# Last pair's g in six buffers, other places for the passes' first loads, and one rounding moved in the first paired step

## The chip, the cores and the metric

The kernel runs on one core of one Trainium2 chip. The time is device microseconds of one execution. Three runs of the kernel before took 910.87, 908.1 and 909.05 us, so the median is 909.05 us.

## The reference

Windowed attention (4 heads with a plain window of 32 keys, 4 with a dilated one), then a dense layer pair without any gating by experts:

```python
def _moe_ref(x, w_in, w_out):
    h = x @ w_in                                              # 4608 x 512 by 512 x 2048
    sp = np.maximum(h, 0.0) + np.log1p(np.exp(-np.abs(h)))    # softplus
    g = h * erf(sp)
    return (g @ w_out).astype(np.float32)                     # by 2048 x 512

def reference(**kwargs):
    attn_out = _attn_ref(q, k, v)          # B, H, S, D = 8, 8, 576, 64
    x = attn_out.transpose(0, 2, 1, 3).reshape(B * S, H * D)
    return _moe_ref(x, w_in, w_out)
```

Inputs and output are float32.

## The kernel before

Matrix products in float32 are made of three products of rounded parts: a value is split into `hi` (rounded) and `lo` (the residue), and hi·hi + hi·lo + lo·hi is summed in PSUM. A cast makes `hi` (mostly on ACT), a subtraction on DVE makes `lo`.

The 4608 tokens are nine chunks of 512. Attention runs in the first part, between the dense work of chunks 0 to 2, and its rest beside the first pair. Chunks 3 to 8 are taken in three pairs, A and B. A pair's first product x·w_in is done by seven block products in place of eight (sums and differences of blocks on both sides), in eight *steps* d of 256 features; seven products a step of six matmuls each. `mm1_big` issues product k, and `take_big` adds its result from PSUM into the step's four half tiles: A's and B's g buffers, of two halves of 512 columns each. Product 0 is copied by ACT into A's second half (L806); products 1 to 6 are added on DVE (L804 and, for both halves of B at once, L816). Then ACT makes softplus (L829) and erf (L1182), and DVE multiplies (L833): the buffer then holds g.

For the first two pairs the steps run in `period`, interleaved with the second product g·w_out of older items (24 matmuls in four quarters, L642), with what is left of attention and with the preparation of x's block sums; `third` issues a group of products. `split_item` rounds an item's g into `ghi` and `glo`. The first paired step is period 0.

The last pair's eight steps (d = 16 to 23, called steps 0 to 7 here) run in `final`, with nothing interleaved on PE. Their g goes to DRAM: A's to a tensor `ga`, B's to one of the tensors `g`, one step later (`store_g`, issued from ACT's queue). The product's operands on the left are loaded two steps ahead by `load_left` (win<-ws, in two parts). Small jobs for later stand in two tables: `LATE` (at a step's end) and `HALFWAY` (after its fifth product).

`rest_steps` then does the second product of the last two items of the pair before ("rest items": 48 matmuls), and `store` writes that chunk from the four PSUM banks `acc`. The last pair's own second product is done by `sums_step`, sixteen *passes* s, again with seven block products (42 matmuls of 256 columns a pass). Each pass needs a half tile of g from two steps: `load_e` fetches it back, `row_sums` makes the block sums on DVE, `operands` rounds them (L1112 on ACT, L968 on DVE). Operands of pass s + 2 are made during pass s, and the load for pass s + 4 is issued at its end. The right-hand block sums of w_out (tensors `wd`) are loaded by `load_sums(p)`, p = 0 to 6; pass s uses p = 2(s mod 4) and the one after it.

Everything runs in the order in which the code issues it (`manual_schedule`): each engine and each DMA queue works its list from the front, and an instruction that waits holds all behind it. SP's queue carries all loads and the output; ACT's queue carries the stores of the last pair's g. Pools hand out buffers in turn: a new tile of a name waits until the tile that had its buffer `bufs` allocations ago is no longer used, also by a store that still reads it. Names that matter: `hc` (two buffers of 1024 columns), `slab(0)` and `slab(1)` (the tiles dbl0 and dbl1 as such buffers), `ghi` and `glo` (two of 512 each), `w` (four of 512).

Before, `pair_of` gives the last pair's even steps the two slabs and its odd ones the two `hc`, so a buffer comes again after two steps. Pass 0 is loaded into two `w` at the end of step 2, pass 1 into slab(1) at the end of step 7, and pass 2 into an `hc` after all matmuls of the rest items.

## Time and profile before

| | |
|---|---|
| median of three runs | 909.05 us |
| the profiled execution, own time | 912.83 us |
| its span, first to last instruction | 911.0 us |
| mean granted clock of PE | 0.985 |
| PE busy | 873.6 us |
| DVE busy | 696.4 us |
| ACT busy | 609.3 us |
| DMA | 193.02 MB, mean 212 GB/s |

A row of the timeline has the start, the duration, the engine, the source line, the operation, out<-in by the program's names and the count of merged instructions; in brackets stand the idle time of the engine ahead of it and what ended that. Matmuls are pipelined, so the start-to-start distance is what a matmul costs. Rows of the chain of work that ended last have a start, a duration and who held it: an engine with its line, a DMA, or "issue". Rows of the table by windows have the window, its length, the busy time of PE, the weight loads, DVE, ACT and POOL with counts, then PE's granted clock (1.00 is full speed), the busy share of the sixteen DMA engines and GB/s. The span by stage: first paired step at 355 us, last pair's steps from 713 us, rest items from 804 us, passes from 815 us.

### The profile page before, as it was taken

How to read it: one execution, taken by the hardware profiler on the slowest of the kernel's cores; microseconds unless marked ns; L12 is line 12 of the kernel's file. 1: busy time of each engine (PE TensorE's matmuls, PEld its weight loads, DVE VectorE, ACT ScalarE, POOL GpSimd, SP SyncE). 2: the span in 40 equal slices, each digit the busy share in tenths (PEclk: the TensorE clock that was granted, in tenths of full speed). 3: DMA queues.
4: the chain of work that ended last, by engine and by line, in shares of the span. 5: the costliest groups of instructions: out<-in, count | busy, mean ns of one | idle time of the engine just before them, and what ended most of it. 6: DMA issues, size and time to landing. Idle time of an engine off the chain costs nothing.

```text
span 911.0 us, 21918 instructions
## 1 busy us (share of the span) xinstructions
PE 873.6 (96%) x8410; PEld 715.4 (79%) x8422; DVE 696.4 (76%) x1748; ACT 609.3 (67%) x1356; POOL 78.6 (9%) x97
## 2 busy tenths in 40 slices
PE   7789999999999999999999999999999988896998
PEld 3467888888888888788888888888888866686998
DVE  5788988887788788686677765868887667675885
ACT  6889989887887887466758525664665456663442
POOL 2212101111111110000110000000000000000000
PEclk9899999999999999999999999999999999997999
DMA  7874436562858887466666825566686388858331
GB/s 277 283 252 147 146 124 209 182 201 89 273 184 304 299 301 241 164 226 219 223 208 229 306 82 188 206 207 196 214 287 250 100 291 271 292 199 301 117 122 64
DMA packets 82568, 193.02 MB, mean 212 GB/s; under 512 B 8992, under 2 KB 25632, under 8 KB 79392
## 3 DMA queue, kind: packets, MB, share of 16 engines
q1 hardware_dynamic: 80160, 183.24, 59.7%
q10 hardware_dynamic: 2304, 8.39, 2.3%
q8 instruction: 66, 1.08, 0.5%
q14 instruction: 38, 0.31, 0.1%
HBM read 133.92 MB, written 57.67 MB: 210 GB/s over the span
## 4 chain that ended last, share of the span: by engine, by line
PE 81%; DMA 9%; DVE 4%; ACT 4%; issue 2%; SPq 1%; POOL 0%; DVEq 0%; ACTq 0%; POOLq 0%
PE acc L642 31%; PE h L796 8%; PE tx L796 8%; PE h L527 7%; PE tx L527 7%; PE acc L1135 4%; PE sp L796 3%; PE sp L281 3%; PE sp L223 2%; PE sp L1135 2%; DMA g<-hc 2%; DMA g<-dbl 2%; DMA ga<-hc 2%; DMA v<-in_v_dram 1%; PE sp L262 1%
## 5 line engine op out<-in xcount | busy, mean ns | idle before, releaser
L642 PE MATMUL acc<-wout_hi,ghi 128*128 128x512 f32 x448 | 177.6, 396 | 0.0
L642 PE MATMUL acc<-wout_lo,ghi 128*128 128x512 f32 x448 | 175.0, 391 | 0.0
L642 PE MATMUL acc<-wout_hi,glo 128*128 128x512 f32 x448 | 124.6, 392 | 0.0
L257 POOL TENSOR_TENSOR prob<-prob,rinv 128x256 f32<-128x256 f32 x72 | 72.0, 1006 | 476.5 <-DVE ssum L255 240.5
L244 ACT ACTIVATE prob<-prob,nmax 128x64 f32<-128x64 f32 x288 | 96.4, 338 | 10.9 <-DVE nmax L234 10.6
L642 PEld LDWEIGHTS acc<-wout_hi,glo 128*128 128x128 f32 x448 | 84.7, 189 | 18.1
L642 PEld LDWEIGHTS acc<-wout_hi,ghi 128*128 128x128 f32 x448 | 84.3, 188 | 17.0 <-DVE ghi L617 0.4
L642 PEld LDWEIGHTS acc<-wout_lo,ghi 128*128 128x128 f32 x448 | 84.4, 188 | 16.8
L234 DVE CUSTOM_DVE_ANT_0 prob<-sp,cst 128x64 f32<-128x64 f32 x288 | 45.2, 220 | 42.5 <-ACT rows L323 29.1
L829 ACT ACT_TABLE_LOAD x26 | 33.4, 1283 | 54.9 <-DVE dbl L804 28.8
L796 PE MATMUL tx<-win 128*128 128x512 f32 x216 | 55.8, 394 | 0.4 <-DVE dbl L816 0.4
L796 PE MATMUL h<-win 128*128 128x512 f32 x216 | 55.7, 393 | 0.0
L244 ACT ACTIVATION_READ_ACCUMULATOR prob<-prob,nmax 128x1 f32 x288 | 54.7, 190 | 0.0
L527 PE MATMUL h<-x,win 128*128 128x512 f32 x192 | 48.7, 396 | 0.0
L527 PE MATMUL tx<-x,win 128*128 128x512 f32 x192 | 48.0, 392 | 0.0
L796 PEld LDWEIGHTS tx<-win 128*128 128x128 f32 x216 | 39.9, 188 | 9.6 <-DVE dbl L816 0.8
L323 ACT COPY rows<-sp 128x128 f32<-128x128 f32 (+7 forms) x167 | 27.6, 309 | 29.7 <-PE sp L223 29.3
L796 PEld LDWEIGHTS h<-win 128*128 128x128 f32 x216 | 39.9, 188 | 9.2 <-DVE dbl L806 0.7
L829 ACT ACTIVATE s<-dbl 128x1024 f32<-128x1024 f32 x24 | 25.4, 1060 | 27.9 <-DVE dbl L804 27.8
L527 PEld LDWEIGHTS h<-x,win 128*128 128x128 f32 x192 | 35.4, 188 | 8.0
L527 PEld LDWEIGHTS tx<-x,win 128*128 128x128 f32 x192 | 35.7, 188 | 7.5
L281 PEld LDWEIGHTS sp<-pT,v 64*64 64x64 f32 x1824 | 29.4, 134 | 11.1 <-DVE s L611 4.6
(311 smaller groups left out, 1948.9 us busy)
## 6 DMA issues: line engine op xcount, KB each, us to landing
win<-ws SPq DMA_DIRECT2D x24, 1024.0 KB, 5.5
v<-in_v_dram SPq DMA_DIRECT2D x72, 256.0 KB, 5.3
win<-ws SPq DMA_DIRECT2D x24, 768.0 KB, 5.8
qk<-in_qk_dram SPq DMA_DIRECT2D x48, 272.0 KB, 5.0
dbl<-in_w_in_dram SPq DMA_DIRECT2D x16, 512.0 KB, 4.0
dbl<-in_w_out_dram SPq DMA_DIRECT2D x16, 512.0 KB, 4.0
ws<-x SPq DMA_DIRECT2D x32, 256.0 KB, 4.9
win<-wd SPq DMA_DIRECT2D x14, 512.0 KB, 7.9
```

The costliest lines, as they stand in the source:

```text
L223: nc.tensor.matmul(sps[h][r * STRIP:(r + 1) * STRIP, i, p, :], qkz[i][hs, s * STRIP:(s + 1) * STRIP], qkz[i][hs, at:at + KEYS], start=True ...
L234: nc.vector.tensor_tensor_reduce(out=pr[:, g, :], in0=sps[h][:, u % 2, p, :], in1=mask[QUADS.index(kinds(u, p))], scale=-SCALE, scalar=HUG ...
L244: nc.scalar.activation(out=probs[u][:, j, :], in_=probs[u][:, j, :], func=AF.Exp, scale=-1.0, bias=nmax[:, j:j + 1], accum_out=sums[u][:, ...
L257: nc.gpsimd.tensor_tensor(probs[u], probs[u], rinv.broadcast_to([P, 2 * PARTS, KEYS]), op=ALU.mult)
L262: nc.tensor.transpose(out=turn_place(u)[:, h * P:(h + 1) * P], in_=pr[:, PARTS * h:PARTS * (h + 1), :].rearrange("p a k -> p (a k)"), iden ...
L281: nc.tensor.matmul(xp[h * D:(h + 1) * D, qs], vt[ks, s, h, :], pt[ks, h * P + s * STRIP:h * P + (s + 1) * STRIP], start=True, stop=True, t ...
L323: nc.scalar.copy(out=to, in_=src)
L527: nc.tensor.matmul((h, bank)[j], win_at[:, ftp, j, cc // 2, w, cc % 2, :], x[cc], start=(k == 0 and i == 0), stop=(k == CC - 1 and i == 2))
L642: nc.tensor.matmul(args["out"], args["lhsT"], args["rhs"], start=args["start"], stop=args["stop"])
L796: nc.tensor.matmul(bank_, w[:, wi, c, :], x[c][:, xi, :], start=(c == 0 and n == 0), stop=(c == 1 and n == 2))
L829: nc.scalar.activation(out=ls[kind_, d], in_=hs[kind_, d], func=AF.Softplus)
L1135: nc.tensor.matmul(y, x[:, at_], w, start=(q == 0 and j == 0 and n == 0), stop=(q == QUART - 1 and j == 1 and n == 2))
```

## The change

Three things change.

1. **Six buffers.** `pair_of` gives the last pair's steps in turn the slabs, the `hc` pair, and four separate tiles of 512 columns, `ghi` twice for A and `glo` twice for B (steps 2 and 5). For these, softplus, multiply and store are issued in halves, and product 5 is added in two instructions.
2. **The passes' first loads.** Pass 0's load, sums and operands come a step later, its operands partly halfway in a step, and the load of the rest items stands halfway in step 6. Pass 1 is loaded into two `w` halfway in step 7. Pass 2 is loaded into slab(1) while the rest items are multiplied. The chunk that the rest items end is written from two `w`, `o` and a `glo`. Later passes go round slab(1), slab(0) and the two `hc` in another order.
3. **First paired step.** The residue of B22 (`LO["B22"]`, two subtractions) is issued ahead of products 4 and 5; the multiply of item NT - 1 and the rounding of its first half come behind them.

```diff
-    def store(c):
+    def store(c, outs=None):
...
-            if c == 0:
+            if outs:
+                o = outs[tt]
+                copy_for(tt)(out=o, in_=acc[tt])
+            elif c == 0:
...
+    def seg(e, j):
+        return e[j] if isinstance(e, list) else e[:, j]
+    def spans(e, *others):
+        if isinstance(e, list):
+            return [(e[j], *(o[:, j] for o in others)) for j in range(PAIR)]
+        return [(e, *others)]
...
+        elif k == 5 and isinstance(hs["B", d], list):
+            add(b0, b0)
+            add(b1, b1)
...
     def pair_of(d):
-        if d % 2:
+        if d >= FIN * SPC and (d - FIN * SPC) % 3 == 2:
+            return [[work.tile([P, TOK], F32, name=n) for _ in range(PAIR)] for n in ("ghi", "glo")]
+        if (d - FIN * SPC) % 3 if d >= FIN * SPC else d % 2:
             return [work.tile([P, PAIR, TOK], F32, name="hc") for _ in range(2)][::-1]
         return [slab(i) for i in range(2)]
...
-            nc.scalar.activation(out=ls[kind_, d], in_=hs[kind_, d], func=AF.Softplus)
+            for e, l in spans(hs[kind_, d], ls[kind_, d]):
+                nc.scalar.activation(out=l, in_=e, func=AF.Softplus)
...
     def store_g(kind_, d, queue):
-        queue.dma_start(out=kept_g[kind_, d // SPC][d % SPC], in_=hs[kind_, d])
+        for e, g in spans(hs[kind_, d], kept_g[kind_, d // SPC][d % SPC]):
+            queue.dma_start(out=g, in_=e)
...
-        if i == 0:
-            multiply(NT - 1)
-        elif behind_ is not None and not ended:
+        if behind_ is not None and not ended:
             multiply_big("A", behind_)
...
-        if ahead is not None:
+        if ahead is not None and i:
             split_item(ahead, 0)
+        if i == 0:
+            jobs(AFT.get((i, 2), ()))
...
         third(2)
-        jobs(AFT.get((i, 2), ()))
+        if i == 0:
+            multiply(NT - 1)
+            split_item(ahead, 0)
+        else:
+            jobs(AFT.get((i, 2), ()))
...
     def room_e(s):
-        return work.tile([P, PAIR, TOK], F32, name="hc") if s % 2 else slab(1 - s // 2 % 2)
+        return slab(s % 2) if s % 4 in (1, 2) else work.tile([P, PAIR, TOK], F32, name="hc")
...
-    LATE = {0: [(sub_split, 6), (sub_store, 6)], 1: [(sub_whole, 7)], 2: [(sub_sums, 7), (load_e, 0, room_halves)],
-            3: [(row_sums, 0, room_w)], 4: [(operands, 0, 0), (operands, 0, 1)],
-            5: [(operands, 0, 2), (operands, 0, 3), (load_rest,)], 6: [(load_sums, 0), (load_sums, 1)],
-            7: [(load_e, 1, lambda: slab(1)), (load_sums, 2), (load_sums, 3)]}
-    HALFWAY = {7: [(split_rest, 0, 0), (split_rest, 0, 1)]}
+    LATE = {0: [(sub_split, 6), (sub_store, 6)], 1: [(sub_whole, 7)], 2: [(sub_sums, 7)],
+            3: [(load_e, 0, room_halves)], 4: [(row_sums, 0, room_w)], 5: [(operands, 0, 1)],
+            6: [(load_sums, 0), (load_sums, 1)], 7: [(load_sums, 2), (load_sums, 3)]}
+    HALFWAY = {5: [(operands, 0, 0)], 6: [(operands, 0, 2), (operands, 0, 3), (load_rest,)],
+               7: [(split_rest, 0, 0), (split_rest, 0, 1), (load_e, 1, room_halves)]}
...
                 load_sums(4)
+                load_e(2, lambda: slab(1))
...
-        load_e(2, lambda: work.tile([P, PAIR, TOK], F32, name="hc"))
-        store(done(REST[-1]))
+        store(done(REST[-1]), [io.tile([P, TOK], F32, name="w", bufs=4) for _ in range(2)] +
+              [small.tile([P, DM], F32, name="o", bufs=1), work.tile([P, TOK], F32, name="glo")])
         load_sums(5)
         load_sums(6)
```

What this does to the order is seen at three places. A row has the source line, the operation, out<-in and what it waits for: DMAHW is a transfer, the others are engines. Line numbers of the change are those of its own file.

ACT around the start of step 2, before (L806 is the copy of a step's first product, L1182 erf, L829 softplus; dbl_8669 is slab(0), dbl_8670 slab(1)):

```order
L806 COPY dbl_8669<-sp_90 128x512 [waits DMAHW5_49,PE_49]
L1182 ACT_TABLE_LOAD
L1182 ACTIVATE s<-s 128x1024 [waits Activation_49] x2
L839 DMA ga<-hc 128x1024 [waits DMAHW1_49,DVE_49]
L829 ACT_TABLE_LOAD [waits DVE_49]
L829 ACTIVATE s<-dbl_8669 128x1024 [waits Activation_49]
L839 DMA g_114<-hc 128x1024 [waits DMAHW4_49,DVE_49]
L829 ACTIVATE s<-dbl_8670 128x1024 [waits DVE_49,Activation_49]
L806 COPY hc<-tx 128x512 [waits DMAHW1_49,PE_49]
```

And now:

```order
L818 COPY ghi<-sp_90 128x512 [waits PE_49]
L1206 ACT_TABLE_LOAD
L1206 ACTIVATE s<-s 128x1024 [waits Activation_49] x2
L859 DMA ga<-hc 128x1024 [waits DMAHW1_49,DVE_49]
L848 ACT_TABLE_LOAD
L848 ACTIVATE s<-ghi 128x512 [waits Activation_49]
L848 ACTIVATE s<-ghi 128x512 [waits DVE_49]
L859 DMA g_114<-hc 128x1024 [waits DMAHW3_49,DVE_49]
L848 ACTIVATE s<-glo 128x512 [waits DVE_49,Activation_49]
L848 ACTIVATE s<-glo 128x512
L818 COPY dbl_8741<-tx 128x512 [waits DMAHW5_49,PE_49]
```

Step 2's copy goes to a `ghi` and waits for PE alone; step 3's copy goes to slab(0) and waits for step 0's store (DMAHW5), no longer for step 1's; softplus comes in halves.

SP's queue from the last load of sums that stands ahead of the output (win<-wd), before (L1051 is a load for a pass, L680 the output):

```order
L1031 DMA win<-wd 128x1024 [waits DMAHW7_49,PE_49]
L1051 DMA hc<-ga 128x2x256 [waits DMAHW4_49,DMAHW0_49,DVE_49]
L1051 DMA hc<-ga 128x2x256 [waits DMAHW1_49]
L680 DMA out_dram<-o 128x512 [waits DMAHW2_49,DVE_49]
L680 DMA out_dram<-w 128x512 [waits DMAHW3_49,Activation_49]
L680 DMA out_dram<-w 128x512 [waits DVE_49]
L680 DMA out_dram<-w 128x512 [waits DMAHW5_49,Activation_49]
L1031 DMA win<-wd 128x1024 [waits DMAHW6_49,PE_49]
```

And now (dbl_9160 is slab(1)):

```order
L1055 DMA win<-wd 128x1024 [waits DMAHW1_49,PE_49]
L1075 DMA dbl_9160<-ga 128x2x256 [waits DMAHW5_49,DMAHW3_49,DVE_49]
L1075 DMA dbl_9160<-ga 128x2x256
L683 DMA out_dram<-w 128x512 [waits DMAHW6_49,DVE_49]
L683 DMA out_dram<-w 128x512 [waits DMAHW7_49,Activation_49]
L683 DMA out_dram<-o 128x512 [waits DMAHW0_49,DVE_49]
L683 DMA out_dram<-glo 128x512 [waits DMAHW1_49,Activation_49]
L1055 DMA win<-wd 128x1024 [waits DMAHW2_49,PE_49]
```

The place in the queue is the same; the buffer that pass 2's load waits for is another one, left by step 6 and not by step 7.

DVE in the first paired step, before (L804 and L816 take products 4 and 5, L740 makes the residue of B22, L266 copies the turned probabilities that the values on PE need):

```order
L611 TENSOR_TENSOR hc<-hc,s 128x1024 [waits Activation_49]
L617 CAST ghi<-hc 128x512 [waits DVE_49,PE_49]
L618 TENSOR_TENSOR glo<-hc,ghi 128x512 [waits DVE_49,PE_49]
L804 TENSOR_TENSOR dbl_5089<-h,dbl_5090 128x512 [waits PE_49]
L816 TENSOR_TENSOR dbl_5090<-tx,dbl_5090 128x1024 [waits DVE_49,PE_49]
L740 TENSOR_TENSOR dbl_5067<-dbl_5067 128x512 [waits DMAHW3_49,DMAHW1_49,Activation_49]
L740 TENSOR_TENSOR plain<-plain 128x512 [waits DMAHW4_49,DMAHW2_49,Activation_49]
L266 COPY pT_87<-sp_90 128x256 [waits PE_49]
```

And now:

```order
L743 TENSOR_TENSOR dbl_5067<-dbl_5067 128x512 [waits DMAHW3_49,DMAHW1_49,Activation_49]
L743 TENSOR_TENSOR plain<-plain 128x512 [waits DMAHW4_49,DMAHW2_49,Activation_49]
L816 TENSOR_TENSOR dbl_5089<-h,dbl_5090 128x512 [waits DVE_49,PE_49]
L832 TENSOR_TENSOR dbl_5090<-tx,dbl_5090 128x1024 [waits DVE_49,PE_49]
L611 TENSOR_TENSOR hc<-hc,s 128x1024
L617 CAST ghi<-hc 128x512 [waits DVE_49]
L618 TENSOR_TENSOR glo<-hc,ghi 128x512 [waits DVE_49]
L266 COPY pT_87<-sp_90 128x256 [waits PE_49]
```

The two residues and the two takes moved ahead of the multiply and the rounding; what comes before and after is the same.

More of the change, by code (lines that the diff above doesn't have):

```diff
@@ L802, in take_big @@
             hs["A", d], hs["B", d] = pair_of(d)
-        a, b = hs["A", d], hs["B", d]
+        (a0, a1), (b0, b1) = ([seg(hs[kind_, d], j) for j in range(PAIR)] for kind_ in "AB")
         add = lambda out, to: nc.vector.tensor_tensor(out=out, in0=y, in1=to, op=ALU.add)
         if k == 0:
-            (nc.scalar.copy if d >= FREED else nc.vector.tensor_copy)(out=a[:, 1], in_=y)
+            (nc.scalar.copy if d >= FREED else nc.vector.tensor_copy)(out=a1, in_=y)
         elif k == 1:
-            add(a[:, 0], a[:, 1])
+            add(a0, a1)
         elif k == 2:
-            add(b[:, 0], a[:, 1])
+            add(b0, a1)
         elif k == 3:
-            add(b[:, 1], b[:, 0])
+            add(b1, b0)
         elif k == 4:
-            add(a[:, 1], b[:, 1])
+            add(a1, b1)
+        elif k == 5 and isinstance(hs["B", d], list):
+            add(b0, b0)
+            add(b1, b1)
         elif k == 5:
+            b = hs["B", d]
             nc.vector.tensor_tensor(out=b, in0=y.rearrange("p (j n) -> p j n", j=1).broadcast_to([P, PAIR, TOK]),
@@ L818, in take_big @@
         else:
-            add(b[:, 0], b[:, 0])
+            add(b0, b0)
     def pair_of(d):
-        if d % 2:
+        if d >= FIN * SPC and (d - FIN * SPC) % 3 == 2:
+            return [[work.tile([P, TOK], F32, name=n) for _ in range(PAIR)] for n in ("ghi", "glo")]
+        if (d - FIN * SPC) % 3 if d >= FIN * SPC else d % 2:
             return [work.tile([P, PAIR, TOK], F32, name="hc") for _ in range(2)][::-1]
@@ L828, in argument_big @@
             ls[kind_, d] = work.tile([P, PAIR, TOK], F32, name="s")
-            nc.scalar.activation(out=ls[kind_, d], in_=hs[kind_, d], func=AF.Softplus)
+            for e, l in spans(hs[kind_, d], ls[kind_, d]):
+                nc.scalar.activation(out=l, in_=e, func=AF.Softplus)
     def multiply_big(kind_, d):
-        e = hs[kind_, d]
-        nc.vector.tensor_tensor(out=e, in0=e, in1=ls[kind_, d], op=ALU.mult)
+        for e, l in spans(hs[kind_, d], ls[kind_, d]):
+            nc.vector.tensor_tensor(out=e, in0=e, in1=l, op=ALU.mult)
         gs[kind_, d] = []
```

## The prediction

> **What bounds the kernel now.** I began with the page's first part and went on to the waits of PE, the timeline of PE where they lie, and the chain that ended last.
>
> ```profile
> PE 873.6 (96%) x8410; PEld 715.4 (79%) x8422; DVE 696.4 (76%) x1748; ACT 609.3 (67%) x1356; POOL 78.6 (9%) x97
> ```
>
> PE is busy for 873.6 of 911.0 us, so only its idle time and its slow stretches can be won. The waits of PE from 700 us to the end are led by these (us in total, times, longest):
>
> ```profile
> PE tx L796 <- ACT hc L806: 4.3, 2, 2.2
> PE h L1135 <- ACT rows L1112: 4.1, 1, 4.1
> PE sp L1135 <- DMA win<-wd: 2.0, 1, 2.0
> ```
>
> They lie in two stretches. L796 is the last pair's eight final steps; L1135 is the passes. The final steps in the timeline of PE, their second product, the next two, two of the waits, and the first matmul behind the last step:
>
> ```profile
> 714.75 1.52 PE L796 MATMUL tx<-win 128*128 128x512 f32 x6
> 716.11 2.88 PE L796 MATMUL sp<-win 128*128 128x512 f32 x12
> ...
> 751.43 1.65 PE L796 MATMUL tx<-x,win 128*128 128x512 f32 x6 [2.24 <-ACT hc L806]
> ...
> 798.02 2.93 PE L796 MATMUL tx<-x,win 128*128 128x512 f32 x6 [2.11 <-ACT hc L806]
> ...
> 803.79 0.39 PE L642 MATMUL acc<-wout_hi,ghi 128*128 128x512 f32 x1
> ```
>
> A product takes 716.11 - 714.75 = 1.36 us. Fifty-five products lie between 714.75 and 803.79: 74.8 of 89.0 us. So **14.2 us** are lost here. What PE waits for is ACT's copy of a step's first product into its g buffer, and the chain says what that copy waits for, a store:
>
> ```profile
> 743.28 7.43 DMA ga<-hc
> ...
> 750.79 0.13 ACT hc L806
> ```
>
> The store of step 1's g lands 7.4 us after its issue, and step 3 wants the same buffer. The second stretch:
>
> ```profile
> 814.67 0.28 PE L1135 MATMUL h<-wout_hi,rows 128*128 128x256 f32 x1
> ...
> 824.55 0.88 PE L1135 MATMUL acc<-win,ghi 128*128 128x256 f32 x6
> ...
> 842.14 0.35 PE L1135 MATMUL h<-wout_hi,plain 128*128 128x256 f32 x1
> ...
> 847.23 0.28 PE L1135 MATMUL acc<-wout_hi,rows 128*128 128x256 f32 x1
> ```
>
> Pass 3 takes 847.23 - 842.14 = 5.09 us. A matmul is 5.09 / 42 = 0.12 us. Pass 2 could begin at 824.55 + 6 x 0.12 = 825.27 and end at 830.36; it ends at 842.14. So **11.8 us** are lost. Its cause is one store in the way of a load, seen in the chain and in SP's timeline:
>
> ```profile
> 813.74 10.31 DMA g<-hc
> ...
> 824.13 1.18 SPq L1051 DMA_DIRECT2D hc<-ga  x2
> ```
>
> Pass 2's operands are loaded into the buffer that the last step's g has to leave first. SP's queue stands until 824.1, with the stores of the output and the last two right-hand sums (win<-wd) behind it.
>
> A third, small place is the first paired step, on PE and on DVE:
>
> ```profile
> 367.84 0.40 PE L642 MATMUL acc<-wout_lo,ghi 128*128 128x512 f32 x1
> ...
> 370.41 0.72 PE L796 MATMUL h<-dbl,win 128*128 128x512 f32 x2 [1.36 <-DVE dbl L740]
> ...
> 374.69 1.14 PE L281 MATMUL sp<-pT,v 64*64 64x32 f32 x64
> ```
>
> ```profile
> 365.28 1.22 DVE L611 TENSOR_TENSOR hc<-hc,s 128x1024 f32<-128x1024 f32 x1
> ...
> 367.74 0.68 DVE L804 TENSOR_TENSOR dbl<-h,dbl 128x512 f32<-128x512 f32 x1
> ...
> 369.67 0.68 DVE L740 TENSOR_TENSOR dbl<-dbl 128x512 fp32r<-128x512 f32 x1
> ...
> 370.87 0.75 DVE L266 COPY pT<-sp 128x256 f32<-128x256 f32 x2
> ```
>
> **The first paired step: 3.3 us.** From 367.84 + 0.23 = 368.07, twelve matmuls (0.227 each, a sixth of a product) would take until 370.8; the next work on PE, the values, began at 374.69, so at most 3.9 us are there, and at worst nothing, if DVE is as late elsewhere. DVE now does the two rounding residues (L740; 370.87 - 369.67 = 1.2 us) from 365.28, then the two takes (1.9 us, from 367.74 to 369.67), by 368.4, then multiply, cast and residue (2.5 us, from 365.28 to 367.74), by 370.9, then the two pT copies that the values need (0.75), by 371.6. The values start at about 371.4, when the first copy is there and the second near its end. I take 3.3. What follows on PE is the same work, shifted.
>
> **The final steps: 13.8 of 14.2 us.** A buffer is now wanted again three steps later instead of two. A step is 7 x 1.36 = 9.52 us. What is late next, once the stores are out of the way, is the ring through DVE and ACT. A step that nothing held up, step 1 (the two multiplies L833 free its predecessor's g for the stores, A and then B):
>
> ```profile
> 729.15 1.22 DVE L833 TENSOR_TENSOR dbl<-dbl,s 128x1024 f32<-128x1024 f32 x1
> ...
> 732.02 1.22 DVE L816 TENSOR_TENSOR hc<-h,hc 128x1024 f32<-128x1024 f32 x1
> ```
>
> Step 1 starts at 714.75 + 6 x 1.36 = 722.91. The store of A can go when L833 ends, 7.5 us in, and lands 15 us in by the 7.43 us above; that of B when L816 begins, 9.1 in. The first copy into that buffer came due with the next step's first product, 9.52 + 1.36 = 10.9 us in, and comes due now at 20.4: 5 us of cover where 4 were missing. The same step's sixth product's bank is free when L816 ends, 10.3 us in; the next step's third product wants it 9.52 + 2.72 = 12.2 us in: 1.9 us of cover. The residues of pass 0's operands that now stand halfway in steps 5 and 6 put 0.8 us (two of 256 columns) and 1.2 us (one of 512, two of 128) of DVE before that take, by the durations in the next fence, and halves instead of a whole tile some 0.15 us: cover 0.6 us and more. The extra stores of a step in halves go in ACT's idle time (it is busy 49.1 of 81 us there, a row below). In step 7 the split of the first rest item writes ghi and glo, which step 5's stores must have left; the last of these is issued about 11 us into step 6 and lands 7.5 later, 9.0 us into step 7, while the first residue is needed 11.3 us in (eight matmuls behind the step). Behind a residue that waits, DVE's queue holds the multiply of B and the last two takes, and behind those ACT holds softplus and the next split. Pass 0's load, sums and operands each come a step later and are used in the passes only: nothing, as each has the 9.5 us of a step. So I leave 0.4 us. Bounds: 14.2, and 9 if each of these covers fails once by 1 to 2 us.
>
> **The passes: 8.8 of 11.8 us.** Pass 2's load keeps its place in SP's queue but goes to a buffer that step 6 leaves, a step earlier; the 10.3 us store is in nobody's way. Loads of later passes go round other buffers, but each still returns after four passes: nothing. Two costs come in. First, pass 1's operands now lie in two halves: eight sums instead of four ahead of the copies that free acc.
>
> ```profile
> 758.59 1.94 DVE L968 TENSOR_TENSOR w<-w 128x128 f32<-128x128 f32 x8
> ...
> 813.63 0.42 DVE L968 TENSOR_TENSOR s<-dbl 128x256 f32<-128x256 f32 x1
> ...
> 815.10 0.68 DVE L968 TENSOR_TENSOR plain<-dbl,plain 128x512 fp32r<-128x512 f32 x1
> ...
> 816.90 0.68 DVE L678 COPY o<-acc 128x512 f32<-128x512 f32 x1
> ```
>
> The four took 815.10 - 813.63 = 1.47 us; eight of half the width take 1.94, and two residues of 256 columns (0.42 each) for the one of 512 at 815.10 add 0.2. The copy ended at 817.58, when PE was just due to write that bank (24 matmuls, 2.9 us, behind 814.67), so this 0.7 us goes to PE. Second, the last right-hand sums. From the load of the rest items halfway in step 6 to the sums that pass 2 needs, about 12 MB move (rest 1, sums 0 to 5 in 6, g stores 3, loads of passes 1 and 2 1, output 1), in the time from 11 us before the rest items' matmuls to 24 us behind their start: 35 us, 343 GB/s. What the queues carry:
>
> ```profile
> 718.00:799.00 81.00, 71.33 (x301) 55.78 (x300) 53.38 (x78) 49.10 (x52) 0.00 (x0) 0.99 0.84 272
> 745.00:751.00 6.00, 3.81 (x16) 2.51 (x14) 3.42 (x6) 2.54 (x4) 0.00 (x0) 1.00 0.91 327
> 796.00:802.00 6.00, 3.98 (x11) 3.16 (x12) 2.79 (x4) 4.59 (x6) 0.00 (x0) 0.72 0.33 134
> 814.00:823.00 9.00, 8.92 (x70) 8.46 (x69) 4.48 (x10) 3.04 (x6) 0.00 (x0) 1.00 1.01 374
> 826.00:841.00 15.00, 8.73 (x37) 8.14 (x38) 9.92 (x29) 6.06 (x15) 0.00 (x0) 0.59 0.99 333
> ```
>
> The last three columns are granted clock, DMA share and GB/s. Full queues carry 333 to 374 GB/s: 32 to 36 us for 35. The last transfer's own way to its landing comes on top, so the sums are 0 to 3.6 us late if I allow 2.6 us for that, the quickest landing among the transfers of this g:
>
> ```profile
> DMA to landing us min/median/max: 2.6/5.6/9.0
> ```
>
> I take 1.5 us of waiting. A wait costs the clock as well: 2.11 us of idle time before 798 us left 0.72 in 796 to 802, though 2.24 us before 751 left 1.00 in 745 to 751. I add 0.8 us. So 11.8 - 0.7 - 1.5 - 0.8 = 8.8; bounds 11.1, and 2.8 if the sums are 3.6 us late and a whole pass runs at half the clock (4.7 us, below). The Trainium skill, page "TensorE: Matmul & The Clock Gate", section "HAM oscillation — how this bites in real kernels", puts the danger at idle gaps above about 3.4 us; by that rule the 0.8 us would fall away. The 2.11 us gap disagrees, the 2.24 us gap agrees.
>
> **The sum.** 3.3 + 13.8 + 8.8 = 25.9 us. The profiled execution took 912.83 us (span 911.0), which would become 886.9. The median of the runs is 909.05, 3.8 us less; against it the same gain gives **883.2 us**.
>
> **Rivals.**
> *The queues become the bound.* The final steps moved 272 GB/s at a share of 0.84, which is 324 at full share; the same bytes in 14 us less ask for 272 x 81/67 = 329. For it: this is the limit just read, and each issue also waits on the semaphore of an older transfer (DMAHW in the order), so that one late landing holds SP's or ACT's queue. Against it: a step's load of win<-ws has more than 13 us from issue to need (it is issued after four or seven products and used two steps later), and its slower half landed in 7.4:
>
> ```profile
> win<-ws SPq DMA_DIRECT2D x6, 768.0 KB, 7.4
> ```
>
> It would cost about 2 us in the final steps and 4 more in pass 2 with its clock: 889.
> *The ring or the split of the rest item is late.* If stores land in 10 us, as the one of 813.74 did, instead of 7.5, the residue comes 1 to 2 us late, the takes behind it too, and so the copies of acc: 2 to 4 us, 886.5.
> *The rotation does not free the copies*, because something else than the buffer held them: then L806 still waits and only the other two terms stay: 897. The chain's store rows speak against it.
> *Slower.* The passes run without a lead. If pass 4's operands land later than about 2 us before pass 4, DVE, 50.1 of 62.9 us busy there, cannot win its lead back, small waits recur in each pass and the clock stays low. At the 0.50 of the second stretch the 42 matmuls of pass 2 were busy for 9.83 us instead of 5.09, 4.7 us more (rows below). Six of the remaining twelve passes at that clock use the gain up; with eight it ends at 921. Against it: at a clock of 1.00 no pass waited from 842.1 on, though DVE had the same work.
>
> ```profile
> 829.50:842.10 12.60, 9.83 (x42) 9.24 (x43) 10.39 (x30) 6.09 (x16) 0.00 (x0) 0.50 0.93 312
> 842.10:905.00 62.90, 62.90 (x526) 62.90 (x525) 50.09 (x114) 26.44 (x50) 0.00 (x0) 1.00 0.32 101
> ```
>
> **Chances.** Forecast (880 to 886) 0.58; queues (886 to 892) 0.24; ring or split (885 to 889) 0.12; no free copies 0.03; slower 0.03. All terms whole would give 909.05 - 28.9 = 880; the range 879.5 to 891 leaves out the last two and the worst of the queues, under 2 in 10. What a measurement of this kernel can tell from no change is about 0.3%, 2.7 us; faster by more than that 0.96, within it 0.01, slower 0.03.
>
> **What would show it.** Right: the rows "L806 COPY" (now another line) without a DMA as releaser, the final steps 76 to 77 us long, no store ahead of pass 2's load, the values of the first paired step close behind its last product. Wrong: a wait of PE on win<-ws, or one at the start of the rest items, waits of several microseconds on win<-wd, or a clock below 1.00 in the passes.

## The result, and the profile after

The changed kernel took 886.47 us (median of 4 runs, 885.91 to 887.33) against 908.67 us of the kernel before beside it (4 runs, 908.1 to 910.87): a ratio of 0.9752, 95% interval 0.9733 to 0.9771, so 22.2 us less. The forecast was 883.2 us in a range of 879.5 to 891.0. The profiled execution took 885.91 us (span 884.1) where the forecast's sum gave 886.9.

The page's first row, and the two rows that are left of PE's waits from 700 us to the end:

```profile
PE 864.0 (98%) x8422; PEld 709.3 (80%) x8422; DVE 696.0 (79%) x1760; ACT 608.1 (69%) x1362; POOL 78.4 (9%) x97
```

```profile
PE sp L1159 <- DMA win<-wd: 1.2, 1, 1.2
PE acc L1159 <- DVE w L670: 0.5, 1, 0.5
```

PE is idle for 20 us instead of 37. (L799 is now the pairs' product, L818 ACT's copy of its first result, L1159 a pass's product, L992 its sums and residues, L852 the multiply, L670 the copies of acc.) The final steps in the timeline of PE, and ACT's copies in them:

```profile
711.61 1.52 PE L799 MATMUL tx<-win 128*128 128x512 f32 x6
...
786.41 0.39 PE L642 MATMUL acc<-wout_hi,ghi 128*128 128x512 f32 x1
```

```profile
731.96 0.57 ACT L818 COPY ghi<-sp 128x512 f32<-128x512 f32 x1
741.43 0.56 ACT L818 COPY dbl<-tx 128x512 f32<-128x512 f32 x1
751.13 0.57 ACT L818 COPY hc<-h 128x512 f32<-128x512 f32 x1
```

From 711.61 to 786.41 are 74.80 us, which is 55 times 1.36: no product waits, where 14.2 us were lost. No copy has a wait in brackets any more. In the passes:

```profile
797.69 0.28 PE L1159 MATMUL h<-wout_hi,rows 128*128 128x256 f32 x1
...
801.23 0.98 PE L1159 MATMUL acc<-win,qk 128*128 128x256 f32 x6 [0.51 <-DVE w L670]
...
803.48 0.28 PE L1159 MATMUL h<-wout_hi,plain 128*128 128x256 f32 x1
...
808.52 0.28 PE L1159 MATMUL h<-wout_hi,rows 128*128 128x256 f32 x1
...
811.70 1.34 PE L1159 MATMUL sp<-win,rows 128*128 128x256 f32 x9 [1.22 <-DMA win<-wd]
...
815.03 0.28 PE L1159 MATMUL h<-wout_hi,plain 128*128 128x256 f32 x1
```

The first matmul of pass 0 is at 797.69, of pass 1 at 803.48, of pass 2 at 808.52, of pass 3 at 815.03. Pass 1 takes 5.04 us, an undisturbed pass. Pass 2 takes 6.51 where it took 12.6 (842.14 - 829.51). Pass 0 waits for the copy of a bank, pass 2 for the last right-hand sums. The chain of work shows where these come from (start, duration, who held it):

```profile
778.29 8.27 DMA g<-glo
786.60 0.14 DVE glo L618 x2
787.25 1.23 DVE dbl L852
788.50 7.70 DMA g<-dbl
796.27 8.94 DMA dbl<-ga
805.28 6.37 DMA win<-wd
```

Read from the top: step 5's store leaves glo, the rest item is split, step 6's g is multiplied and goes to DRAM (7.70 us), comes back for pass 2 (8.94 us), and at 805.28, when that load has landed, the second of the last two loads of sums that pass 2 needs is issued; it lands 6.37 us later. In the first paired step, on PE and on DVE:

```profile
368.92 1.07 PE L642 MATMUL acc<-wout_hi,glo 128*128 128x512 f32 x4
370.21 1.45 PE L281 MATMUL sp<-pT,v 64*64 64x32 f32 x64 [0.22 <-DVE pT L266]
```

```profile
364.28 0.68 DVE L743 TENSOR_TENSOR dbl<-dbl 128x512 fp32r<-128x512 f32 x1
...
367.42 1.22 DVE L611 TENSOR_TENSOR hc<-hc,s 128x1024 f32<-128x1024 f32 x1
...
369.74 0.75 DVE L266 COPY pT<-sp 128x256 f32<-128x256 f32 x2
```

The values begin 0.2 us behind the last product. The residue (L743) is done before the multiply (L611) and nobody waits for either.

### The profile page after: what moved, and what is told of

Its sections match the earlier page's. It is cut to its first block, busy times and chain, and to the rows that moved or that the text cites. A ratio compares the mean times of both kernels' runs of the same rounds, so it can differ in the third digit from the quotient of the medians.

```text
span 884.1 us, 21952 instructions
## 1 busy us (share of the span) xinstructions
PE 864.0 (98%) x8422; PEld 709.3 (80%) x8422; DVE 696.0 (79%) x1760; ACT 608.1 (69%) x1362; POOL 78.4 (9%) x97
## 3 DMA queue, kind: packets, MB, share of 16 engines
q8 instruction: 66, 1.08, 0.5%
## 4 chain that ended last, share of the span: by engine, by line
PE 82%; DVE 8%; DMA 7%; issue 1%; ACT 1%; SPq 0%; POOL 0%; DVEq 0%; ACTq 0%; POOLq 0%
PE acc L642 29%; PE tx L799 9%; PE h L799 9%; PE h L527 7%; PE tx L527 7%; PE sp L799 5%; PE acc L1159 3%; PE sp L281 3%; PE sp L223 3%; PE sp L1159 2%; PE sp L262 1%; DMA qk<-in_qk_dram 1%; PE tx L1159 1%; PE h L1159 1%; DMA dbl<-ga 1%
## 5 line engine op out<-in xcount | busy, mean ns | idle before, releaser
L799 PE MATMUL h<-win 128*128 128x512 f32 x216 | 55.7, 393 | 0.0
L799 PE MATMUL tx<-win 128*128 128x512 f32 x216 | 55.7, 393 | 0.0
L799 PEld LDWEIGHTS h<-win 128*128 128x128 f32 x216 | 39.9, 188 | 9.2 <-DVE dbl L818 0.7
L799 PEld LDWEIGHTS tx<-win 128*128 128x128 f32 x216 | 40.0, 188 | 8.9
L848 ACT ACTIVATE s<-dbl 128x1024 f32<-128x1024 f32 x22 | 23.3, 1061 | 27.4 <-DVE dbl L816 27.3
```

The source lines that it names most:

```text
L799: nc.tensor.matmul(bank_, w[:, wi, c, :], x[c][:, xi, :], start=(c == 0 and n == 0), stop=(c == 1 and n == 2))
L848: nc.scalar.activation(out=l, in_=e, func=AF.Softplus)
```

## The experiments

The table reads each kernel's profile by stages from the timeline of PE. *Paired step*: from its first big product to the next period's second one. *Steps lost*: from the second product of the final steps to the first matmul of the rest items, less 74.8. *Rest*: the rest items. *Pass 0*: to pass 1's first matmul. *Passes 1 and 2 lost*: from there to pass 3's first matmul, less 10.47 us, which is how the prediction came to its 11.8 (22.25 in the kernel before); two undisturbed passes take 2 x 5.04 = 10.08 us, so a reading of -0.4 means that nothing is lost. All in us.

| profile of | paired step | steps lost | rest | pass 0 | passes 1 and 2 lost | pass 3 to the end |
|---|---|---|---|---|---|---|
| before | 21.28 | 14.24 | 10.88 | 5.22 | 11.78 | 68.86 |
| before, second profile | 21.31 | 10.21 | 11.66 | 5.33 | 9.45 | 69.13 |
| six buffers alone | 21.30 | 0.00 | 11.88 | 5.32 | 10.13 | 68.78 |
| first loads alone | 19.75 | 12.90 | 12.52 | 5.79 | 1.39 | 69.50 |
| rounding alone | 18.10 | 12.51 | 12.43 | 5.96 | 11.09 | 68.87 |
| the change | 18.11 | 0.00 | 11.28 | 5.79 | 1.08 | 69.07 |
| the change, second profile | 18.11 | 0.00 | 11.20 | 5.87 | 3.36 | 68.75 |

**The three parts by themselves.** These and the one after them ran on one chip, where the kernel before took 908.96 us (17 runs, 906.52 to 913.43). First the six buffers, with the passes' loads and the paired step as before:

```diff
     def pair_of(d):
+        if d >= FIN * SPC and (d - FIN * SPC) % 3 == 2:
+            return [[work.tile([P, TOK], F32, name=n) for _ in range(PAIR)] for n in ("ghi", "glo")]
```

> Part 1 of the change alone: six buffers, the passes' first loads and the first paired step as before. Theory (the three places add up): the final steps take 76 to 77 us instead of 90 and PE has no wait in them, pass 2 still loses about 12 us to the store ahead of its load; time 895 us, 13 to 14 below before. Rival (the gain is given back behind the steps, because the last step's store then meets the loads of the sums earlier): final steps 76 to 77 us, but pass 2 loses 20 us or more; time 903 us or above.

897.35 us (895.7 to 899.71, 4 runs), ratio 0.9859 (0.9832 to 0.9886): 11.6 us less. PE's waits from 700 us on:

```profile
PE h L1155 <- ACT rows L1132: 3.4, 1, 3.4
PE sp L1155 <- DMA win<-wd: 1.8, 1, 1.8
PE acc L642 <- ACT ghi L617: 1.1, 2, 0.7
```

The steps lose nothing any more, and pass 2 loses as before (10.1), so the rival, which had pass 2 lose 20 us, is out. The gain is short of the 13 to 14 us expected: the steps of the kernel before lose 10 to 14 us by the profile, and up to 1 us goes in the rest items that wait for the split (L617). Then the passes' first loads, with the two-step ring:

```diff
-    HALFWAY = {7: [(split_rest, 0, 0), (split_rest, 0, 1)]}
+    HALFWAY = {5: [(operands, 0, 0)], 6: [(operands, 0, 2), (operands, 0, 3), (load_rest,)],
+               7: [(split_rest, 0, 0), (split_rest, 0, 1), (load_e, 1, room_halves)]}
...
+                load_e(2, lambda: slab(1))
```

> Part 2 alone: the passes' first loads at the new places, four buffers and the first paired step as before. Theory: the final steps still lose about 14 us, pass 2's operands are there, PE loses 1 to 3 us at pass 0's fifth product and at win<-wd; time 898 to 900 us, 9 to 11 below before. Rival (the queues bound pass 2 and not the one store): PE waits 5 us or more on win<-wd in pass 2 with the clock halved; time 904 us or above.

901.59 us (899.42 to 904.6, 6 runs), ratio 0.9907 (0.9882 to 0.9931): 7.4 us less, short of the 9 to 11 expected. Its profile has more waits of another kind in the steps:

```profile
PE sp L799 <- DVE hc L816: 2.1, 1, 2.1
PE sp L799 <- DVE dbl L832: 1.8, 2, 1.4
PE acc L642 <- ACT ghi L617: 1.8, 2, 1.3
```

Passes 1 and 2 lose 1.4 instead of some 10, as expected. In the steps the waits for DVE's takes (L816, L832) have grown and those for ACT's copies have shrunk; the steps lose 12.9 us in all, which lies between the three profiles with the same four buffers (14.24, 10.21 and 12.51). So it is not shown that the jobs that now stand in the steps cost anything there, and where the 1.6 us and more went that are missing stays open; pass 0 (5.79) and the rest items (12.52) are at the long end of the table. Third, the paired step alone:

```diff
+        if i == 0:
+            jobs(AFT.get((i, 2), ()))
...
+        if i == 0:
+            multiply(NT - 1)
+            split_item(ahead, 0)
```

> Part 3 alone: the residue of B22 ahead of products 4 and 5 in the first paired step. Theory: no wait of PE for L740 there, 3.2 us gained in that step, about 1 us of it lost again behind 475 us where the trace of the change shows DVE waiting for the landing of an output store; time 2 to 3 us below before. Rival (PE ahead by 3 us only meets the other engines and transfers later): within 1 us of before.

905.52 us (901.24 to 911.05, 12 runs), ratio 0.9957 (0.9937 to 0.9976): 3.4 us less, 3.18 by the table. The expected 2 to 3 us lie within that interval, and the rival's "within 1 us" doesn't. The unchanged step took 21.3 us in three profiles and 19.75 in that of the first loads, with the same waits of PE for DVE (0.3 and 1.4 us) in it. What differs is the clock behind them, here in the kernel before and in the first loads alone:

```profile
371.00:375.00 4.00, 4.00 (x30) 2.77 (x32) 1.31 (x3) 1.06 (x1) 0.00 (x0) 0.57 0.44 133
```

```profile
371.00:375.00 4.00, 4.00 (x138) 3.23 (x137) 0.87 (x2) 1.39 (x5) 0.00 (x0) 1.00 0.61 195
```

In all three profiles with 21.3 us the clock falls there, and with the residue moved it stays at 1.00. So about 1.5 us of the 3.2 are a fall of the clock that goes with the waits.

The three gains add to 22.4 us, the whole change has 22.2. That fits parts that add up, as the sum assumed, though the intervals of the three (1.8 to 2.5 us each way) would let a few microseconds of overlap pass.

**The sums ahead of pass 2's load.** Is it the place of the last sums in SP's queue, or the bytes ahead of them, that makes pass 2 wait?

```diff
                 load_sums(4)
+                load_sums(5)
                 load_e(2, lambda: slab(1))
...
-        load_sums(5)
         load_sums(6)
```

> The changed kernel with load_sums(5) moved ahead of pass 2's load and of the output's stores in SP's queue. Theory (the 1.2 us wait on win<-wd in pass 2 is a place in the queue): no wait there, time 1 to 1.5 us below the changed kernel. Rival (the queues are full, so that what goes first only delays what goes after): the wait moves to pass 2's operands or to the sums of pass 3, time within 0.5 us of the changed kernel or above it.

888.09 us (887.19 to 889.03, 4 runs), ratio 0.9755 (0.9731 to 0.978). The wait for win<-wd is gone and two others stand there:

```profile
PE h L1159 <- DVE rows L992: 1.0, 1, 1.0
PE tx L1159 <- DVE w L992: 0.6, 1, 0.6
```

The first is pass 2's operands, whose load is now issued later; the second is in pass 4. This is what the rival said: the same bytes in another order, another wait, and a ratio that can't be told from the change's 0.9752.

**A second profile of the kernel before.** The profiled executions differ by 26.9 us (912.83 to 885.91), the medians by 22.2. This and the next three ran on one chip (the kernel before 909.52 us, 17 runs, 906.65 to 913.35).

> The kernel before, a second profile of it. Theory: the first profiled execution (912.83 us, 3.8 above its median) lost more than a usual one at the places that the change touches, so this one, if it lies near 909, loses 12.3 to 13.2 us in the final steps and 10 to 11.3 in pass 2, where the first lost 14.2 and 11.8. Rival: the 3.8 us lie elsewhere (attention, the rest items) and the forecast's gain was too large for another reason: then the steps lose 14 and pass 2 11.6 or more again. Time against the kernel before: 1.000, within 0.3%.

909.09 us (907.16 to 913.62, 12 runs), ratio 1.000 (0.9981 to 1.0019); the profiled execution took 909.13 us. Its waits of PE from 700 us on:

```profile
PE h L1135 <- ACT rows L1112: 4.0, 1, 4.0
PE tx L796 <- ACT hc L806: 3.6, 2, 2.6
PE sp L1135 <- DMA win<-wd: 2.5, 2, 1.7
PE sp L796 <- ACT hc L806: 1.1, 1, 1.1
PE sp L796 <- ACT dbl L806: 1.1, 1, 1.1
```

The same waits in the same places, with other amounts: the steps lost 10.2 us instead of 14.2, passes 1 and 2 9.5 instead of 11.8. Both fall below what the theory named (12.3 to 13.2 and 10 to 11.3), and further from the rival; in these places it lost 6.4 us less, in the others 2.7 more. Over the three profiles that hold both old places (two of before and the rounding alone) steps and passes together lost 26.0, 19.7 and 23.6. The first profile is the worst of them. Late stores are only a part of why. The first profile and then the second read, in the passes,

```profile
826.00:846.00 20.00, 13.73 (x74) 13.14 (x75) 14.89 (x40) 9.12 (x21) 0.00 (x0) 0.66 0.76 255
```

```profile
826.00:846.00 20.00, 15.10 (x108) 14.51 (x109) 16.14 (x43) 10.27 (x24) 0.00 (x0) 0.83 0.74 247
```

The clock is at 1.00 or at 0.50 in shorter windows, so it was at 0.50 for 13.6 of these 20 us in the first and for 6.8 in the second. With the 0.72 from 796 to 802 us, where the second has 1.00, the first spent 17 us at half clock in the two places, the second 7, and the rounding alone 14: the order of their losses. A fall comes behind some waits and not behind others, so like waits cost more in one execution than in another.

**Order of copies, sums and output.** Three kernels move single calls at the start of the passes of the changed kernel. The copies of acc ahead of the fourth pair of operands:

```diff
                 operands(1, 1)
-                operands(1, 2)
         store(done(REST[-1]), [io.tile([P, TOK], F32, name="w", bufs=4) for _ in range(2)] +
...
+        operands(1, 2)
```

> The changed kernel with the copies of acc and their output stores ahead of the fourth pair of casts and residues of pass 1's operands (0.68 us on DVE, 0.5 on ACT). Theory (DVE's queue, with eight half sums, makes the copy late): PE's 0.51 us wait for the copy in pass 0 goes, 0.5 us less in all if nothing else follows, 886.0; the operands come 1.2 us later and have 2 us and more. Rival (pass 2's sums set the end of this stretch, because their landing does not move): the 0.5 us is added to the wait for them, 1.2 becomes 1.7, and the time stays at 886.5.

888.44 us (884.96 to 888.97, 5 runs), ratio 0.9764 (0.9742 to 0.9786). Pass 0 is 0.6 us shorter (5.19), as the theory said, and in pass 2 the timeline of PE shows

```profile
813.11 1.33 PE L1159 MATMUL sp<-win,rows 128*128 128x256 f32 x9 [2.04 <-DMA win<-wd]
```

No gain is seen in the time, as the rival said: pass 2 goes on when the sums land, so what is won ahead of them is waited for. That the wait grew from 1.22 to 2.04 us can't be put down to the edit, since the change itself has 1.94 in a second profile (below). The sums directly behind pass 2's load, ahead of the output:

```diff
+        load_sums(5)
         store(done(REST[-1]), [io.tile([P, TOK], F32, name="w", bufs=4) for _ in range(2)] +
...
-        load_sums(5)
```

> The changed kernel with the sums that pass 2 waits for directly behind pass 2's load and ahead of the four output stores (1 MB). Theory (the sums stand in SP's queue until 804.5 us behind stores that nobody needs soon; in front of them they are issued at about 797.5): they land at about 806 instead of 811.7, the wait of 1.2 us goes, 885.3 or a little less. Rival (the DMA queues are full until 816 us, so what is put ahead delays the rest): the wait moves to pass 2's operands or to pass 3, as it did when the sums stood ahead of pass 2's load, and the time stays within 0.5 us of 886.5.

884.74 us (884.3 to 888.85, 5 runs), ratio 0.9743 (0.9717 to 0.9768). And both edits:

> Both of these edits. Theory of both: pass 0 without its 0.5 us and pass 2 without its 1.2, 884.8. Rival: as for the sums alone, the time stays at 886 to 886.5.

885.79 us (885.51 to 887.63, 4 runs), ratio 0.975 (0.9728 to 0.9771). In both profiles the wait for the sums is gone and pass 4 waits for DVE (1.42 and 1.13 us), so the wait has moved on, the rival's mechanism, if one pass later than it named; with both edits pass 2 waits another 0.66 for its operands. The first median lies at the theory's 885.3 or below, the second between the two; both intervals overlap that of the change, so neither is shown to be faster.

**Bytes taken out of the way, and put in it.** The last group of runs (the kernel before took 909.21 us there, 11 runs, 905.67 to 916.33) begins with the change itself once more,

> The changed kernel again, beside the next three on the same chip. Theory: 886.5 as before, within 1 us; the final steps without a wait of PE; in pass 0 about 0.5 us for the copy of acc and in pass 2 about 1.2 us for the last sums (between 0.5 and 2.5, as landings vary), the granted clock 1.00 where the gap stays near 1 us.

which took 887.68 us (885.27 to 889.45, 6 runs), ratio 0.9764 (0.9737 to 0.9791). Its profiled execution, 889.07 us, is one of its slower ones, with a longer wait in pass 2 and, in the table by windows, a lower clock behind it:

```profile
813.62 1.84 PE L1159 MATMUL sp<-win,rows 128*128 128x256 f32 x9 [1.94 <-DMA win<-wd]
```

```profile
806.00:812.00 6.00, 5.67 (x47) 5.47 (x46) 4.28 (x12) 2.68 (x6) 0.00 (x0) 1.00 0.98 354
812.00:818.00 6.00, 4.38 (x24) 4.38 (x25) 4.86 (x17) 2.83 (x9) 0.00 (x0) 0.72 1.03 379
```

In the first profile of the change the same windows read

```profile
806.00:812.00 6.00, 4.78 (x40) 4.58 (x39) 5.90 (x18) 3.22 (x8) 0.00 (x0) 1.00 1.03 376
812.00:818.00 6.00, 6.00 (x52) 6.00 (x51) 5.59 (x15) 3.98 (x12) 0.00 (x0) 1.00 0.90 321
```

So a gap of 1.22 us left the clock at 1.00 and one of 1.94 was followed by 0.72; passes 1 and 2 took 2.28 us longer than in the first profile, 0.72 of it by the longer wait and 1.56 behind it. Beside it, the output stores behind pass 4's load, which takes 1 MB from ahead of the sums:

```diff
+    out_later = []
...
+            if outs:
+                out_later.append((r, o))
+                continue
...
         load_e(s + 4, lambda: room_e(s + 4))
+        while out_later:
+            r, o = out_later.pop(0)
+            nc.sync.dma_start(out=out[r:r + P, :], in_=o)
```

> The changed kernel with the four output stores of the chunk (1 MB) issued behind pass 4's load instead of ahead of the last two right-hand sums; the copies of acc stay where they are. Theory (full queues: bytes ahead of the sums set their landing): 1 MB at the 404 GB/s of that stretch is 2.6 us, the sums land at about 809 instead of 811.7 and pass 2 begins without the 1.2 us wait; pass 4's operands come no later, since its load is ahead of the output: 885.3. Rival (something is always the last to land there, so that the wait moves on, as in the orders tried so far): a wait of 0.6 to 1.4 us appears at pass 2's operands or in pass 4, and the time is 886 to 887.5.

886.0 us (884.2 to 888.55, 6 runs), ratio 0.9754 (0.9725 to 0.9782). And with the copies first:

> The same, with the copies of acc also ahead of the fourth pair of casts and residues of pass 1's operands. Theory: pass 0 without its 0.5 us and pass 2 still without a wait, since the queues have 2.6 us to give: 884.8. Rival: as for the kernel with the output alone, 886 to 887.5.

887.0 us (883.6 to 888.22, 6 runs), ratio 0.9752 (0.9726 to 0.9779). In both, passes 1 and 2 lose next to nothing (-0.23 and -0.15 in the table's count), as the theory said; but pass 4 takes 6.45 us, where the two profiles of the change have 5.26 and 5.04. That, and the times, are the rival's. The timeline of PE and the windows of the kernel with the output later:

```profile
820.02 0.98 PE L1164 MATMUL tx<-win,rows 128*128 128x256 f32 x6 [0.60 <-DVE w L997]
```

```profile
806.00:812.00 6.00, 6.00 (x51) 5.88 (x51) 5.93 (x18) 3.23 (x9) 0.00 (x0) 1.00 1.04 401
812.00:818.00 6.00, 5.94 (x50) 5.74 (x49) 5.97 (x16) 4.34 (x12) 0.00 (x0) 1.00 0.64 219
818.00:824.00 6.00, 5.32 (x40) 4.76 (x40) 5.77 (x15) 2.00 (x5) 0.00 (x0) 1.00 0.14 48
```

The third number behind the window's length is DVE: 5.93, 5.97 and 5.77 us of 6. It starts on pass 2's operands when their load has landed and is then busy for 17.7 of 18 us; in pass 4 a sum out of a bank (w<-tx, L997) comes behind residues that are late already, and PE waits for the bank. So the wait for the sums had hidden a lateness of DVE of about the same size: from pass 1's first matmul to the end these two kernels take 80.8 us each, and the change 80.6 in its first profile and 82.6 in its second. Last, the output stores twice:

```diff
             (nc.scalar if last and tt % 2 else nc.sync).dma_start(out=out[r:r + P, :], in_=o)
+            if outs:
+                nc.sync.dma_start(out=partial[tt], in_=o)
```

> The changed kernel with each of the four output stores issued a second time, to a tensor that nothing reads (1 MB more ahead of the last two sums). Theory (full queues): the sums land 2.6 us later, PE waits 3.8 us for them in pass 2 instead of 1.2, and the clock falls behind a gap of over 2 us, 1 to 2 us more: 890 to 891. Rival (the queues have room and the sums are late only by where they stand): 8 issues in place of 4 cost about 2 us of SP's queue, the wait grows by that at most and the time stays at or below 888.5.

890.15 us (888.34 to 893.3, 6 runs), ratio 0.9798 (0.9771 to 0.9824), 2.5 us above the change beside it. The timeline of PE in pass 2, and the windows:

```profile
814.20 2.05 PE L1161 MATMUL sp<-win,rows 128*128 128x256 f32 x9 [3.20 <-DMA win<-wd]
```

```profile
806.00:812.00 6.00, 5.00 (x42) 4.80 (x40) 5.59 (x17) 2.91 (x7) 0.00 (x0) 1.00 1.05 408
812.00:818.00 6.00, 3.80 (x19) 3.80 (x20) 3.49 (x10) 2.54 (x8) 0.00 (x0) 0.72 1.04 396
```

The wait is 2.0 us longer than in the first profile of the change and 1.3 longer than in the second, under the 2.6 us that 1 MB takes at 404 GB/s; the time lies in the theory's range. But the theory's mechanism is not what the chains show. The load that pass 2 waits for, here and in the second profile of the change:

```profile
807.82 6.34 DMA win<-wd
```

```profile
807.20 6.38 DMA win<-wd
```

From issue to landing it takes as long as in the first profile (6.37). What moved is the issue: 3.82 us behind pass 1's first matmul (804.00), where the first profile has 1.80 (805.28 - 803.48) and the second 2.58 (807.20 - 804.62). So the wait grew by the time that the load stood in SP's queue, which now held four more stores; that is the rival's mechanism and its size, "about 2 us". The rival's time, 888.5 at most, was too low because it left out the clock (0.72 here). Whether the stores held the queue by their bytes or by their number was not separated: an issue there also waits for older transfers to land.

## Why the prediction was right, and where its size was off

*First paired step, 3.3 us.* 21.28 - 18.11 = 3.2 in the profile, and the part alone brought 3.4 in the runs. The order of events is the one worked out: the copies of pT end at 370.5, the values begin at 370.21. The size was read off the values' old start at 374.69, and about 1.5 us of what lies ahead of it are slow matmuls at half clock, which the prediction did not name here; in an execution without that fall the term is 1.6 us (19.75 - 18.11).

*Final steps, 13.8 of 14.2.* All 14.24 went there. The rest items took 0.40 more (10.88 to 11.28), which is what the prediction had set aside for covers; but the kernel before had 11.66 in its second profile, so this loss is within the spread. The named cover was tight where it was said to be: step 5's last store lands at 778.29 + 8.27 = 786.56, 9.7 us into step 7 (which starts at 776.9), forecast 9.0, and the residue goes through for the first matmul that needs it at 788.22. The ring's cover of 5 us held although stores landed later than the 7.43 us it was worked out with (8.27 and 7.70 in the chain above).

*Passes, 8.8 of 11.8.* The profiled execution lost 1.08 in passes 1 and 2 and 0.57 more in pass 0 (5.79 to 5.22), and pass 3 to the end took 0.2 us longer: 9.9 us won. Forecast for the copy of acc 0.7, waited 0.51; for the last sums 1.5, waited 1.22; for the clock 0.8, nothing. The second profile has 0.59, 1.94 and, by the table's count, 1.4 for the same three. So the terms were right in kind, and their sum, 3.0, lies between the two executions' 1.7 and 4.0. The wait for the sums was sized by a fit of bytes to what the queues carry, and there three things were off. The last transfer's own way, put at 2.6 us, took 6.4. The 12 MB are units of 1,048,576 bytes, so 35 us ask for 360 GB/s and not 343, and at 333 to 374 GB/s they take 34 to 38 us. And the queues carried 404 GB/s at a share of 1.04 (800 to 806 us), more than the 374 that the bounds used. The first two make the sums later and the third earlier. And what moved the landing between the profiles is the time of the issue, as the chains above show, which this sum doesn't hold; that 1.5 lies between 1.22 and 1.94 is in part luck.

*The clock.* A fall behind a short gap costs about 1.5 us (1.56 between the two profiles of the change, 21.30 - 19.75 = 1.55 in the first paired step) or doesn't come; 0.8 was no amount that occurs, but the mean of the two. The rule that the prediction weighed (the Trainium skill, page "TensorE: Matmul & The Clock Gate", section "HAM oscillation — how this bites in real kernels", danger above about 3.4 us) would leave the clock whole behind each of these gaps. The first profile of the change agrees (1.00 behind 1.22 us), the second disagrees (0.72 behind 1.94 us), and so does the first paired step of the kernel before (0.57 over 4 us behind a gap of 1.36 us).

*The sum and the median.* By its own executions the forecast came to 886.9 us and 885.91 was measured: a gain of 26.9 for the 25.9 forecast. The weak step is the last one, "against it the same gain gives 883.2 us". The profiled execution of before was 3.8 us above the median, and it had lost more in the very places that the change removes: 26.0 us in steps and passes, where two other profiles had 19.7 and 23.6. The change takes this whole loss, so the gain of a usual execution is smaller than that of the profiled one. How much smaller, three profiles can't say. With the mean of the three, 23.1, in place of 26.0 the gain is 23.0 and the forecast 886.1 against the measured 886.47; with the 19.7 of the second profile, the only one whose execution (909.13 us) lay at its median, it is 19.6 and 889.5. So the direction is shown and the amount is not. The clock runs through all of it: among the eleven executions of the kernel before in the last group the three with the lowest mean clock, 0.983, took 912.1 to 916.3 us, and the two with the highest, 0.992 and 0.996, 905.7 and 906.7. Some us more vary from run to run elsewhere: the first paired step begins between 353.7 and 356.7 us in the profiles. (A slip without weight: "all terms whole" is 3.3 + 14.2 + 11.8 = 29.3, not 28.9, so 879.8 and not 880.)

*The rivals.* Queues as the bound: not in the final steps (no wait on win<-ws in any profile of the six buffers), but at the start of the passes SP's queue and the landings set the pace, and there every order of the same bytes gave 884.7 to 888.4. The ring or the split late: at most 0.4 us of it, in the rest items. Rotation that frees nothing: excluded by the six buffers alone. Slower, by passes without a lead: its mechanism was seen in small, in pass 4 of the kernels that took the wait for the sums away, 1.2 to 1.4 us in one pass and then caught up; its price of twelve passes was not.

What stays open: whether step 6's way out to DRAM and back (788.50 to 805.2 us in the chain), SP's queue behind it, or DVE's work can be made shorter. No kernel tried that, and of those tried none is shown to be faster than the change.

## What to carry to other kernels

A wait for a buffer that a store still reads goes as a whole when the buffer comes back a step later, and its size can be read off the chain beforehand; but take the size from several profiles, since losses that hang on landings and on the clock vary (26.0, 19.7 and 23.6 us here), and the execution that was profiled may be an unlucky one. Look at the clock in short windows behind each wait: a wait that goes can take 1.5 us of slow matmuls with it, or none. Where several transfers and an engine are late together, as pass 2's sums, its operands and DVE here, removing the wait that shows brings only what it has over the next one; moving calls about in a stretch whose DMA share is 1 moved the wait here, and was not shown to move the end. When a load lands late, look first whether it was issued late: here its way took 6.3 to 6.7 us in four profiles, and its time in SP's queue made most of the difference.

## What the runs showed of the hardware

The granted clock does not follow the length of one gap. Behind gaps of PE of 1.94, 2.04, 2.11 and 3.20 us it read 0.72 in the six-microsecond window, and 0.57 over 4 us behind a gap of 1.36 us in the first paired step. In windows of half a microsecond it reads 1.00 or 0.50 except where it changes, so each of these is about 3.4 us at half clock (0.28 x 2 x 6 and 0.43 x 2 x 4). Behind gaps of 1.22, 2.24 and 2.61 us (the last at 797.00 in the second profile of before), and behind the same 1.36 us in the profile of the first loads, it read 1.00. In the passes of the kernel before (two profiles) and of the rounding alone, with a gap of 4.0 to 4.4 us and shorter ones behind it, the time at half clock is 6.8 to 13.6 us. What decides was not tried.

The sixteen DMA engines moved 404 to 408 GB/s at shares of 1.04 to 1.05; from 788 to 796 us, where step 6's store took 7.70 us to land, they moved 374 at a share of 1.00. The same program's times spread by 4.2 us (the change, six runs on one chip) and 10.7 us (the kernel before, eleven runs there), while the second product of the final steps begins between 710.5 and 713.0 us in the change and its variants. That fits a loss of the kernel before which varies in the stretch that the change repairs; it does not show it.
